# VectorE in written order while the expert weights are prepared, an expert every 9 clock units, and preference for the early steps of ten chunks

## The chip, the core and the metric

The kernel runs on one core of a Trainium2 chip. That core has five engines with instruction streams of their own: TensorE (PE, matrix products), VectorE (DVE), ScalarE (ACT), GpSimd (POOL) and SyncE (SP, which mostly issues transfers). The streams meet only through semaphores. The metric is the time of one execution on the device, in microseconds (us); smaller is better.

## What is computed

A softmax over seven taps weights a causal sum over the sequence, for each of 8 heads. The result goes through a mixture of 8 experts, one expert a token.

```python
# x (8, 3584, 192), weight_gen (8, 3584, 8 heads, 7 taps)
w = np.exp(weight_gen - np.max(weight_gen, axis=-1, keepdims=True))
w = w / (np.sum(w, axis=-1, keepdims=True) + 1e-09)
out = np.einsum('bshk,bskhg->bshg', w, x_unf)   # x_unf: the last 7 rows of each token
...
# x is now out as (28672, 192); w_gate (192, 8), w1 (8, 192, 1024), w2 (8, 1024, 192)
logits = x @ w_gate
expert_idx = np.argmax(logits, axis=1)
gate_w = softmax(logits)[np.arange(N), expert_idx]
for e in range(E):
    h = np.maximum(x_sorted[lo:hi] @ w1[e], 0.0)
    y_sorted[lo:hi] = h @ w2[e]
return gate_w[:, None] * y
```

## The kernel before

The 28672 tokens are cut into 28 chunks of 1024 (8 tokens in each of 128 partitions). A chunk goes through these steps:

- **sums** (L660): softmax of the tap weights (`soft0` to `soft3`) and the weighted sum. For chunks 0 to 2 VectorE makes the products of six of the eight token columns (L354, 1152 wide) and PE adds them up in PSUM by a product with the identity (L363), while POOL does the other two columns alone. From chunk 3 on VectorE does products (L354) and additions (L378) of all columns, 13 passes of 1536.
- **split** (L640): `high` rounds the sum to 16 bits on ACT (L444 or L448) and `low` forms the rest (L461 and L463 on VectorE, or L451 to L453), then 24 transposes on PE (L473), copied out by ACT (L475).
- **finish** (L647): the gate's logits on PE (L485), read by VectorE (L492) and reduced to the expert choice (`route1`, up to L507), ranks on PE (L512, L514), `gate` and `places` on VectorE (L521 to L544), and the scatter of the 1024 rows to the experts' queues in DRAM by POOL (L559). At last `choose` (L568 to L605) selects which full tiles of which expert are ready. Its row numbers are read by SP.

An expert tile (`experts`, L754) reads rows of one expert by a transposing transfer (L743) and that expert's prepared weights, 1.8 MB (L745), and does two layers on PE (L805, L711) with ACT and VectorE between them. Tiles of chunks 1 to 4 have 256 rows: 1 is ready behind chunk 1 and 4 each behind chunks 2, 3 and 4. From chunk 6 on a tile has 384 rows. Tiles come in a fixed order, 97 in all. In the tiles of chunks up to 4 VectorE has no part (L814 and L820 on ACT); later it has one in two tiles of three (L828).

Before the first tile the weights of all experts are prepared, three experts in flight (`PROB` = 3). An expert's raw weights are loaded (L239 to L242), their norms formed on PE (L261) and reduced on VectorE (L262), which is `w_norm`. `w_high` sums over partitions on PE (L268), makes the scale on VectorE (L209 to L212, L270) and the 16-bit part on ACT (L271, L272). `w_low` makes the remainder on VectorE (L278, L280), stores all to `wq` in DRAM (L285 to L290) and then loads the expert three further on into the same buffers. Their memory is given to the tiles' buffers afterwards, and a tile's weights come from `wq`, so no tile starts before the last expert is stored.

The order of the program is written by one loop with a clock of its own, `vector_step` (L907): it takes the next due piece of the tiles' VectorE work, of the weights (`weights`, L868: expert e is due at `W_AT + W_GAP * e`, its later steps 4 and 8 units later), of a chunk's finish, of its split, or else of the sums. A framework then builds the instruction streams from that program. Inside `tc.manual_schedule` with VectorE named, VectorE keeps the written order. Outside, and for all other engines, a scheduler may put a later instruction first when its model finds the earlier one not ready; `tc.high_priority()` gives the instructions inside it preference in that choice. Before the change the stage of the weights (L958) is outside, and the tiles' stage (L960 on) inside; preference goes to the finish of every chunk (`route`) and to nothing else.

Of the kernel before, what the change touches and what calls it, by code (L numbers as in the profile page):

```python
# [46 lines left out]
SHRINK = 1.0 - 2.0 ** -11  # L47
FETCH = 16.0
W_AT = 10.0
W_GAP = 11.0  # L50
W_HIGH = 4.0
W_LOW = 8.0
T_MAIN = 384
# [3 lines left out]
EXP_AT = 4  # L57
SC_AT = 7
MX_FROM = 3
SQ = 4  # L60
PROB = 3
TV = 2
# [51 lines left out]
def conv_moe_kernel(ctx: ExitStack, tc: tile.TileContext, x, wgen, w_gate, w1, w2, out):  # L114
# [203 lines left out]
    def soft0(c):  # L318
        k = ch[c]
        mx = cw.tile([P, J * H], F32, name="mx")  # L320
        nc.vector.tensor_reduce(mx, k.w, axis=AX.X, op=ALU.max)  # L321
        nc.gpsimd.tensor_tensor(k.w, k.w, mx.unsqueeze(2).to_broadcast([P, J * H, KW]), op=ALU.subtract)  # L322

    def soft1(c):
        nc.scalar.activation(ch[c].w, ch[c].w, AF.Exp)
# [80 lines left out]
    def square(c, n, m):  # L406

        k = ch[c]

        def one(half, i, col, m):  # L410
            junk = cw.tile([P, m * D], BF16, name="junk", bufs=1, padded_shape=[P, J * D])
            v = k.x[:, col:col + m, :].rearrange("p a d -> p (a d)")
            nc.scalar.activation(junk, v, AF.Square, accum_out=ssqs[:, half, i:i + 1])  # L413

        if c == 0 and n == 0:
            one(1, 0, 0, HALO)
        one(c % 2, n // 2, HALO + n, m)
# [242 lines left out]
    def sums():  # L660
# [9 lines left out]
        for c in range(NCH):  # L670
# [4 lines left out]
            for cost in taps(c):  # L675
                n += 1
                if n <= 2 and c + 1 < NCH:
                    for i in range(4 * n - 4, 4 * n, SQ):
                        square(c + 1, i, SQ)
                yield cost, None  # L680
                if c + 1 < NCH:
                    if n == 2 and c + 1 < MX_FROM + 2:
                        soft0(c + 1)
                        yield 0.6, None
                    if n == EXP_AT:
                        soft1(c + 1)
                    if n == MX_AT and MX_FROM <= c < NCH - 2:

# [179 lines left out]
    def weights(pro):  # L868

        ev = []  # L870
        for e in range(E):
            at = W_AT + W_GAP * e
            ev += [(at, e, 0), (at + W_HIGH, e, 1), (at + W_LOW, e, 2)]
# [15 lines left out]
    wstream = [None, 0.0]  # L889
# [2 lines left out]

    def advance(queue_, what, after):
        at, g, c = queue_[0]
        with tc.high_priority() if what == "route" else nullcontext():
            lat = next(g, None)
        if lat is None:
            done[what] = c
            queue_.pop(0)
            if after:  # L900
                after(c)
        else:
            lat, cost = lat if isinstance(lat, tuple) else (lat, OP)
            clock[0] += cost
            queue_[0][0] = clock[0] + lat

    def vector_step():  # L907
# [12 lines left out]
        if routes and routes[0][0] <= now + (HURRY if routes[0][2] < SOON else 0.0):  # L920
            clock[0] = max(now, routes[0][0])
            advance(routes, "route", None)
            return True
# [22 lines left out]
    with tc.tile_pool(name="pro", bufs=PROB) as pro, tc.tile_pool(name="pro1", bufs=1) as pro1:  # L946
        stats = [pro1.tile([P, 2], F32, name=f"st{e}") for e in range(E)]
        stage = [pro1.tile([P, W_STAGE], F16, name=f"ws{i}") for i in range(PROB)]
        for t in stage:
            nc.gpsimd.memset(t[:, W_INV:W_INV + 16], 0.0)  # L950
        load(0)
        for e in range(len(stage)):
            w_load(e, pro)
            if e == 0:
                load(1)
        wstream[0] = weights(pro)
        clock[0] = 5.0
        while wstream[0] is not None:  # L958
            vector_step()
    with tc.manual_schedule(engines={mybir.EngineType.DVE}):  # L960
        ffw = ctx.enter_context(tc.tile_pool(name="ffw", bufs=3, reuse_waits="tile"))
        ffx = ctx.enter_context(tc.tile_pool(name="ffx", bufs=2, reuse_waits="tile"))
# [41 lines left out]
```

## Time and profile before

| | |
|---|---|
| median of 3 runs | 1240.84 us (1239.42 to 1244.1) |
| the profiled execution | 1242.18 us, span 1240.5 us |
| PE busy | 1133.4 us, 91% of the span |
| VectorE busy | 1036.7 us, 84% |
| ACT, POOL busy | 696.8 us, 660.6 us |
| mean DMA rate | 259 GB/s over the span |

Busy PE means that some product was in its pipeline, not that it ran at its peak. The span counts from the first instruction that the profile shows to the last; the time of an execution has some 1.7 us more. The chain that ended last lies on PE for 63% of the span and on VectorE for 13%. In the profile's slices of 31 us PE stands at 2 and 1 tenths from 93 to 155 us. The rows used are in the section on the trace below.

### The profile page before, as it was taken

To read this page: it belongs to the slowest core of one execution; us is meant where nothing else is said; L and a number is where in the kernel's file an instruction comes from. 1 tells how busy PE (TensorE), PEld (TensorE's weight loads), DVE (VectorE), ACT (ScalarE), POOL (GpSimd) and SP (SyncE) were. 2 spreads that over 40 slices of the span, in tenths; PEclk is the share of its full clock that TensorE was granted. 3 is DMA by queue.
4 is the path that set the end of the run, shared out by engine and by line. 5 is a ranking of instruction groups with operands and counts; after the bars stand their busy time and mean duration, and the time that the engine had idled before them with its cause. 6 is when DMAs were issued, how large, how long until landed. Compare 5 with 4: busy or idle time off the path is not lost.

```text
span 1240.5 us, 30087 instructions
## 1 busy us (share of the span) xinstructions
PE 1133.4 (91%) x11621; PEld 927.2 (75%) x11621; DVE 1036.7 (84%) x1849; ACT 696.8 (56%) x1459; POOL 660.6 (53%) x562
## 2 busy tenths in 40 slices
PE   5692189997999999999999999999999998999997
PEld 3461179896678788778788787787777786789997
DVE  7999966999999999999999999999998976232331
ACT  3455167675566666656756666656655663543442
POOL 6850853666656565446755565656464656222222
PEclk9896599999999999999999999999999999999998
DMA  9996698897768878787798878878776667999995
GB/s 277 346 323 241 232 282 264 287 304 236 232 201 267 265 230 250 238 234 235 247 277 237 237 227 255 247 240 254 239 215 178 191 197 222 340 348 348 321 362 218
DMA packets 185133, 320.93 MB, mean 259 GB/s; under 512 B 132752, under 2 KB 156434, under 8 KB 169118
## 3 DMA queue, kind: packets, MB, share of 16 engines
q1 hardware_dynamic: 162862, 273.68, 70.8%
q0 software_dynamic: 22128, 45.33, 11.1%
q8 instruction: 91, 1.49, 0.5%
q14 instruction: 52, 0.43, 0.1%
HBM read 236.17 MB, written 60.76 MB: 239 GB/s over the span
## 4 chain that ended last, share of the span: by engine, by line
PE 63%; DVE 13%; DMA 10%; issue 7%; POOL 4%; SPq 1%; ACT 1%; POOLq 0%; DVEq 0%; ACTq 0%
PE ph L805 29%; PE y L711 27%; DVE tv L354 4%; DVE acc L378 3%; DMA wt<-wq 3%; PE ph L473 2%; PE ph L818 2%; DMA f<-in_moe_w_dram 2%; POOL out_dram L559 2%; DMA xt<-queue 2%; DMA queue<-pl,pos 2%; DVE hl L828 1%; POOL queue L559 1%; PE ph L363 1%; PE pm L485 1%
## 5 line engine op out<-in xcount | busy, mean ns | idle before, releaser
L805 PE MATMUL ph<-xt,wt 128*128 128x384 f16 (+6 forms) x3880 | 578.8, 292 | 24.5 <-DMA wt<-wq 16.8
L711 PE MATMUL y<-wt,hh 128*128 128x192 f16 (+2 forms) x3696 | 504.5, 247 | 2.1 <-ACT o L715 2.1
L559 POOL DMA_INDIRECT out_dram<-o,meta x231 | 288.5, 1249 | 394.6 <-ACT o L715 349.0
L711 PE MATMUL y<-wt,hl 128*128 128x192 f16 (+2 forms) x1848 | 450.3, 247 | 0.4 <-ACT hl L820 0.2
L805 PEld LDWEIGHTS <-wt 128*128 128x128 f16 x3880 | 329.3, 98 | 144.4 <-DMA wt<-wq 18.9
L711 PEld LDWEIGHTS <-hh 128*128 128x128 f16 (+2 forms) x3696 | 337.0, 99 | 35.9 <-issue 5.0
L559 POOL DMA_INDIRECT queue<-pl,pos x224 | 286.8, 1280 | 118.1 <-issue 56.7
L828 DVE SCALAR_TENSOR_TENSOR hl<-ph,hh 128x384 f16<-128x384 f32 (+2 forms) x372 | 204.2, 562 | 144.2 <-ACT hh L825 139.0
L354 DVE TENSOR_TENSOR tv<-x_sb,wp 128x1536 f32<-128x1536 f32 (+1 forms) x171 | 289.0, 1693 | 3.9 <-PE ph L363 3.7
L825 ACT ACTIVATE hh<-ph 128x384 f16<-128x384 f32 (+2 forms) x372 | 185.5, 501 | 181.0 <-PE ph L805 170.4
L378 DVE TENSOR_TENSOR acc<-acc,tv 128x1536 f32<-128x1536 f32 x150 | 261.8, 1745 | 0.0
L711 PEld LDWEIGHTS <-hl 128*128 128x128 f16 (+2 forms) x1848 | 181.7, 98 | 16.5 <-ACT hl L820 1.4
L814 ACT ACTIVATE hh<-ph 128x384 f16<-128x384 f32 (+1 forms) x204 | 105.2, 518 | 84.7 <-PE ph L805 82.0
L715 ACT ACTIVATE o<-y,fac 128x192 f32<-128x192 f32 (+2 forms) x231 | 91.7, 418 | 89.4 <-PE y L711 83.4
L820 ACT ACTIVATE hl<-ph 128x384 f16<-128x384 f32 (+1 forms) x204 | 104.1, 519 | 37.0 <-PE ph L818 36.4
L475 ACT ACTIVATE xg<-ph 128x1024 f16<-128x1024 f16 x84 | 83.9, 1027 | 24.3 <-PE ph L473 24.2
L473 PE MATMUL ph<-idh,pl 128*128 128x128 f16 x672 | 56.1, 225 | 25.4 <-ACT pl L448 15.8
L818 PE MATMUL ph<-hh,negi 128*128 128x384 f16 (+1 forms) x256 | 68.1, 304 | 1.7 <-ACT hh L814 1.6
L473 PEld LDWEIGHTS <-pl 128*128 128x128 f16 x672 | 44.5, 101 | 29.4 <-ACT pl L448 16.1
L363 PE MATMUL ph<-tv,identf 128*128 128x384 f32 x126 | 51.6, 553 | 7.6 <-DVE tv L354 7.3
L413 ACT ACTIVATE junk<-x_sb 128x768 bf16<-128x768 f32 (+2 forms) x56 | 48.0, 857 | 13.6 <-DMA x_sb<-in_x_dram 6.5
L322 POOL TENSOR_TENSOR w_sb<-w_sb,mx 128x448 f32<-128x448 f32 x28 | 29.7, 1062 | 45.5 <-DVE mx L321 43.6
(121 smaller groups left out, 780.7 us busy)
## 6 DMA issues: line engine op xcount, KB each, us to landing
wt<-wq SPq DMA_DIRECT2D x97, 1796.0 KB
x_sb<-in_x_dram SPq DMA_DIRECT2D x27, 1344.0 KB
w_sb<-in_weight_gen_dram SPq DMA_DIRECT2D x28, 224.0 KB
wq<-ws SPq DMA_DIRECT2D x8, 772.0 KB
f<-in_moe_w_dram SPq DMA_DIRECT2D x8, 768.0 KB
f<-in_moe_w_dram SPq DMA_DIRECT2D x8, 512.0 KB
wq<-ws SPq DMA_DIRECT2D x8, 512.0 KB
wq<-ws SPq DMA_DIRECT2D x32, 128.0 KB
```

Of the source, the lines that this page charges most:

```text
L354: eng.tensor_tensor(out, xs, ws, op=ALU.mult)
L378: eng.tensor_tensor(ac, ac, t, op=ALU.add)
L473: nc.tensor.transpose(pt[:, m, :], p16[:, j, n * P:(n + 1) * P], idh)
L559: st = nc.gpsimd.indirect_dma_start(out=dst, out_offset=bass.IndirectOffsetOnAxis(ap=idx, axis=0), in_=src, in_offset=None, **kw)
L711: nc.tensor.matmul(y, hx[:, f, sl], w2v[:, f, t, :], start=(f == 0 and k == 0), stop=(f == NF - 1 and k == 2))
L715: nc.scalar.activation(o[0:m, :], y, AF.Copy, scale=fac[0:m, s:s + 1])
L805: nc.tensor.matmul(ph[:, g], wt[:, wc + f * P:wc + (f + 1) * P], xt[:, xc, 0:T], start=(k == 0 and g == 0), stop=(k == 4), skip_group_chec ...
L814: nc.scalar.activation(hv, ph, AF.Relu, scale=SHRINK)
L818: nc.tensor.matmul(ph[:, g], negi, hv[:, g], start=False, stop=True, skip_group_check=True)
L820: nc.scalar.activation(lv, ph, AF.Relu)
L825: nc.scalar.activation(hv, ph, AF.Relu)
L828: nc.vector.scalar_tensor_tensor(lv, ph, 0.0, hv, op0=ALU.max, op1=ALU.subtract)
```

## The change

Three things change: `W_GAP` goes from 11 to 9 units of the loop's clock, so that the expert's steps are due earlier between the chunks' steps; the stage of the weights goes under `tc.manual_schedule` for VectorE, so that VectorE keeps the written order there too; and the split of chunks 0 to 9 gets the preference that the finish had alone. The finish had it already for all chunks.

```diff
--- before.py
+++ after.py
@@ -47,7 +47,7 @@
 SHRINK = 1.0 - 2.0 ** -11
 FETCH = 16.0
 W_AT = 10.0
-W_GAP = 11.0
+W_GAP = 9.0
 W_HIGH = 4.0
 W_LOW = 8.0
 T_MAIN = 384
@@ -57,6 +57,7 @@
 EXP_AT = 4
 SC_AT = 7
 MX_FROM = 3
+FRONT = 10
 SQ = 4
 PROB = 3
 TV = 2
@@ -892,7 +893,7 @@
 
     def advance(queue_, what, after):
         at, g, c = queue_[0]
-        with tc.high_priority() if what == "route" else nullcontext():
+        with tc.high_priority() if what == "route" or c < FRONT else nullcontext():
             lat = next(g, None)
         if lat is None:
             done[what] = c
@@ -955,8 +956,9 @@
                 load(1)
         wstream[0] = weights(pro)
         clock[0] = 5.0
-        while wstream[0] is not None:
-            vector_step()
+        with tc.manual_schedule(engines={mybir.EngineType.DVE}):
+            while wstream[0] is not None:
+                vector_step()
     with tc.manual_schedule(engines={mybir.EngineType.DVE}):
         ffw = ctx.enter_context(tc.tile_pool(name="ffw", bufs=3, reuse_waits="tile"))
         ffx = ctx.enter_context(tc.tile_pool(name="ffx", bufs=2, reuse_waits="tile"))
```

In the built programs VectorE has the same instructions. From the last row of chunk 3's choose on, its list is the same in both; ahead of that the same rows stand in another order. The line numbers of the changed program are one higher behind line 59, two higher at the end.

On VectorE, the stretch in which the logits of chunk 0 are read (`lg`, L492 before, L493 after; `ws` rows are an expert's remainder, `st` its norms, `tv` conv products, `pl` a chunk's payload). Before, expert 3's rows and two conv chunks lie around and between the steps:

```order
L278 SCALAR_TENSOR_TENSOR ws_177<-f_358,nsc,ws_177 128x1536
L343 TENSOR_TENSOR wp<-w_sb,sm 128x336
L492 TENSOR_REDUCE lg<-pm 128x64
L280 SCALAR_TENSOR_TENSOR ws_177<-f_359,nsc,ws_177 128x8x192
L354 TENSOR_TENSOR tv<-x_sb,wp 128x1152
L461 TENSOR_TENSOR pl_133<-acc,pl_133 128x2x128
L463 TENSOR_TENSOR pl_133<-acc,pl_133 128x2x64
L495 TENSOR_REDUCE lm<-lg 128x8
L354 TENSOR_TENSOR tv<-x_sb,wp 128x1152
L262 TENSOR_REDUCE st_173<-y 128x2
L497 TENSOR_TENSOR lg<-lg,lm 128x64
```

After the change the same read stands right behind expert 1's two rows and expert 2's norms:

```order
L355 TENSOR_TENSOR tv<-x_sb,wp 128x1152 x2
L279 SCALAR_TENSOR_TENSOR ws_178<-f_200,nsc,ws_178 128x1536
L281 SCALAR_TENSOR_TENSOR ws_178<-f_201,nsc,ws_178 128x8x192
L263 TENSOR_REDUCE st_171<-y 128x2
L493 TENSOR_REDUCE lg<-pm 128x64
L496 TENSOR_REDUCE lm<-lg 128x8
L498 TENSOR_TENSOR lg<-lg,lm 128x64
L502 SCALAR_TENSOR_TENSOR pri<-lg,revE 128x64
L210 TENSOR_SCALAR nbits<-y 128x2
L212 TENSOR_SCALAR nsc<-nbits 128x2
L213 TENSOR_SCALAR nin<-nbits 128x2
```

The read of chunk 0's logits moved from behind expert 3's L278 to behind expert 1's L281, and its following steps stand next to each other with expert 2's scale among them.

On VectorE, the end of the weights' stage (`f_943` and `f_854` are the raw weights of the last expert). Before, the conv passes of chunk 3 (`acc`) are finished and chunk 4's have begun:

```order
L278 SCALAR_TENSOR_TENSOR ws_178<-f_942,nsc,ws_178 128x1536
L378 TENSOR_TENSOR acc<-acc,tv 128x1536
L343 TENSOR_TENSOR wp<-w_sb,sm 128x448
L584 TENSOR_TENSOR eq<-cand,top 1x64
L497 TENSOR_TENSOR lg<-lg,lm 128x64
L280 SCALAR_TENSOR_TENSOR ws_178<-f_943,nsc,ws_178 128x8x192
L354 TENSOR_TENSOR acc<-x_sb,wp 128x1536
L587 TENSOR_TENSOR eq<-eq,rowc 1x64
L600 TENSOR_SCALAR cand<-cand,top 1x64
L501 SCALAR_TENSOR_TENSOR pri<-lg,revE 128x64
```

After, chunk 3 has begun its conv only, chunk 2's payload stands before the last expert's rows and its logits behind them:

```order
L355 TENSOR_TENSOR acc<-x_sb,wp 128x1536
L462 TENSOR_TENSOR pl_133<-acc,pl_133 128x2x128
L464 TENSOR_TENSOR pl_133<-acc,pl_133 128x2x64
L468 TENSOR_TENSOR lsc<-isx,nin 128x1
L322 TENSOR_REDUCE mx<-w_sb 128x64
L355 TENSOR_TENSOR tv<-x_sb,wp 128x1536 x2
L279 SCALAR_TENSOR_TENSOR ws_178<-f_853,nsc,ws_178 128x1536
L281 SCALAR_TENSOR_TENSOR ws_178<-f_854,nsc,ws_178 128x8x192
L493 TENSOR_REDUCE lg<-pm 128x64
L496 TENSOR_REDUCE lm<-lg 128x8
```

Ten conv passes of chunk 3 moved behind the last expert's rows, and chunk 1's choose in front of them.

On ACT, the copies of the first chunk that comes after the first expert tile has begun (`hh`, `hl` and `o` belong to tiles, `fac` stands once in each tile). Before, this is chunk 4 (`pl_132`), in the third tile:

```order
L325 ACTIVATE w_sb<-w_sb 128x448
L715 ACTIVATE o<-y,fac 128x192
L820 ACTIVATE hl<-ph 128x2x256
L842 ACTIVATE fac<-meta,wt 128x2
L814 ACTIVATE hh<-ph 128x2x256
L448 ACTIVATE pl_132<-acc 128x4x192 x2
L814 ACTIVATE hh<-ph 128x2x256 x2
```

After, it is chunk 3 (`pl_131`), in the second tile:

```order
L821 ACTIVATE hl<-ph 128x2x256 x3
L326 ACTIVATE w_sb<-w_sb 128x448
L815 ACTIVATE hh<-ph 128x2x256 x2
L716 ACTIVATE o<-y,fac 128x192
L821 ACTIVATE hl<-ph 128x2x256 x2
L449 ACTIVATE pl_131<-acc 128x4x192 x2
L716 ACTIVATE o<-y,fac 128x192
```

Chunk 3's copies moved from ahead of the first tile into the second; chunk 4's, further on, moved from behind 2.25 tiles to behind 5. On PE the ranks of chunk 3 stand behind 3.0 tiles (none before), those of chunk 4 behind 7.25 (5.33), of chunk 5 behind 9.75 (8.22), of chunk 6 behind 11.75 (11.05), and of chunk 7 behind 13.5 in both.

## Rows read from the trace of the kernel before

**Rows 1.** The profile's page, busy tenths of TensorE and VectorE in 40 equal slices of 31.0 us.

```profile
PE   5692189997999999999999999999999998999997
...
DVE  7999966999999999999999999999998976232331
```

**Rows 2.** The table by stretch: from and to in us, length, then busy time and number of instructions of PE, PE's weight loads, VectorE, ACT and POOL, and last the granted clock of PE as a share of full speed, the DMA share and GB/s. Eleven stretches of 31 us, and one short stretch from another such table.

```profile
0.00:31.00 31.00, 16.54 (x82) 10.94 (x82) 22.42 (x52) 10.79 (x16) 20.12 (x46) 1.00 0.92 277
31.00:62.00 31.00, 21.18 (x113) 12.67 (x112) 30.78 (x40) 15.32 (x26) 25.29 (x24) 0.84 1.02 346
62.00:93.00 31.00, 28.98 (x211) 19.13 (x210) 29.37 (x52) 16.79 (x26) 15.66 (x14) 0.99 1.01 323
93.00:124.00 31.00, 7.02 (x105) 5.80 (x103) 31.00 (x52) 16.44 (x23) 2.98 (x4) 0.67 0.69 241
124.00:155.00 31.00, 4.79 (x66) 4.03 (x66) 30.41 (x72) 5.02 (x7) 26.36 (x16) 0.50 0.67 232
155.00:186.00 31.00, 27.87 (x264) 24.42 (x264) 20.14 (x20) 18.91 (x39) 15.50 (x15) 0.95 0.95 281
186.00:217.00 31.00, 30.67 (x350) 28.60 (x351) 21.19 (x39) 22.55 (x44) 9.50 (x8) 1.00 0.88 265
217.00:248.00 31.00, 28.57 (x330) 26.41 (x328) 29.30 (x46) 20.51 (x41) 21.50 (x15) 1.00 0.85 285
248.00:279.00 31.00, 30.45 (x350) 28.26 (x349) 29.63 (x48) 22.50 (x45) 20.01 (x16) 1.00 0.93 305
279.00:310.00 31.00, 22.23 (x248) 18.73 (x247) 29.99 (x52) 17.58 (x36) 19.83 (x16) 0.92 0.80 237
310.00:341.00 31.00, 28.90 (x259) 21.38 (x256) 31.00 (x56) 17.29 (x36) 18.74 (x13) 0.92 0.71 233
...
57.00:60.00 3.00, 3.00 (x5) 1.77 (x6) 3.00 (x4) 0.00 (x0) 2.92 (x4) 0.50 0.95 272
```

**Rows 3.** The timeline of PE: start and duration in us, engine, line and operation, output<-inputs, number of instructions in the row, and in brackets the idle time before it and what ended that. L363 are the conv taps that go through PE, L261 the norms of one weight half, L805 the first layer of an expert tile.

```profile
23.75 2.18 PE L363 MATMUL ph<-tv,identf 128*128 128x384 f32 x6
...
56.92 6.95 PE L363 MATMUL ph<-tv,identf 128*128 128x384 f32 x12 [3.00 <-DVE tv L354]
...
100.78 0.86 PE L261 MATMUL y<-f 128*128 128x128 bf16 x12 [0.57 <-DMA f<-in_moe_w_dram]
...
155.27 5.08 PE L805 MATMUL ph<-xt,wt 128*128 128x256 f16 x32 [9.99 <-DMA wt<-wq]
...
201.08 1.26 PE L805 MATMUL ph<-xt,wt 128*128 128x256 f16 x10
```

**Rows 4.** The timeline of VectorE, with the same columns. L280 is the last weight row of an expert (expert 1 and expert 7 here), L605 the last row of chunk 3's choose, L461 the first row of chunk 4's low part, L492 the read of a chunk's logits (chunk 4 at 196, chunk 7 at 288 us).

```profile
47.86 2.63 DVE L280 SCALAR_TENSOR_TENSOR ws<-f,nsc,ws 128x1536 f16<-128x1536 f32 x1
...
127.75 1.80 DVE L280 SCALAR_TENSOR_TENSOR ws<-f,nsc,ws 128x1536 f16<-128x1536 f32 x1
...
148.88 0.15 DVE L605 SCALAR_TENSOR_TENSOR posn<-cnt,posn 1x8 f32<-1x8 f32 x1
...
177.52 0.69 DVE L461 TENSOR_TENSOR pl<-acc,pl 128x512 f16<-128x512 f32 x1 [10.76 <-ACT pl L448]
...
196.15 0.29 DVE L492 TENSOR_REDUCE lg<-pm 128x64 f32<-128x128 f32 x1 [9.81 <-PE pm L485]
...
288.10 0.29 DVE L492 TENSOR_REDUCE lg<-pm 128x64 f32<-128x128 f32 x1 [1.01 <-PE pm L485]
```

**Rows 5.** VectorE's groups by line and shape from 0 to 155 us: names, shapes, count, then busy us and mean ns of one, and idle time before them.

```profile
L354 DVE TENSOR_TENSOR tv<-x_sb,wp 128x1152 f32<-128x1152 f32 x21 | 28.2, 1346 | 3.8 <-PE ph L363 3.7
L354 DVE TENSOR_TENSOR tv<-x_sb,wp 128x1536 f32<-128x1536 f32 x11 | 19.2, 1744 | 0.0
...
L378 DVE TENSOR_TENSOR acc<-acc,tv 128x1536 f32<-128x1536 f32 x9 | 15.7, 1739 | 0.0
...
L330 DVE TENSOR_REDUCE sm<-w_sb 128x64 f32<-128x448 f32 x5 | 3.0, 611 | 0.0
```

**Rows 6.** The timeline of SP's queue (issues of transfers, with the time that an issue took). L285 is the first store of an expert's prepared weights (expert 0 here), L286 one of the last (expert 7 here), L242 the last load of an expert's raw weights (expert 3 and expert 7), L743 the read of a tile's rows, L745 of its weights.

```profile
31.34 0.40 SPq L285 DMA_DIRECT2D wq<-ws  x1
...
39.82 0.56 SPq L242 DMA_DIRECT2D f<-in_moe_w_dram  x1
...
91.91 0.66 SPq L242 DMA_DIRECT2D f<-in_moe_w_dram  x1
...
129.97 0.38 SPq L286 DMA_DIRECT2D wq<-ws  x1
144.14 1.33 SPq L743 DMA_TRANSPOSE xt<-queue  x1
145.95 0.39 SPq L745 DMA_DIRECT2D wt<-wq  x1
```

**Rows 7.** The timeline of POOL: the first scatter of chunk 1 and the last of chunk 3, of 24 that follow each other.

```profile
124.07 6.35 POOL L559 DMA_INDIRECT queue<-pl,pos  x1 [8.74 <-ACT ws L272]
...
166.83 0.96 POOL L559 DMA_INDIRECT queue<-pl,pos  x1 [0.30 <-issue]
```

**Rows 8.** The chain of work that ended last, in two stretches: start and duration in us, and what. The first two rows are the landing of chunk 2's scatters and the read of the second tile's rows; the third is the first layer of the eighth tile.

```profile
155.36 5.98 DMA queue<-pl,pos
161.34 3.18 DMA xt<-queue
...
228.01 2.25 PE ph L805 x19
```

## The prediction

> **What bounds the kernel now.** I read the slices of the page first [rows 1]: TensorE (PE) is nearly empty in the fourth and fifth slice (93 to 155 us) and stays at 8 or 9 from the eleventh to the last but one, while VectorE (DVE) is full from the second to the fifth. The table by stretch says it in numbers [rows 2]: from 93 to 155 us PE works 11.8 of 62 us and DVE 61.4. No expert product runs before 155.27 us [rows 3]. From 155 to 341 us PE idles 17.3 us (six rows summed); DVE idles 20.7 us in the first two of these rows and 4.1 us in the other four. So three stretches follow each other: DVE's front, a middle in which DVE sets the pace after two waits of its own, and PE's long run. The end moves by as much as the start of the long run moves.
>
> One milestone is enough to measure that. From the last row of chunk 3's choose (L605) on, DVE's list is the same row for row in both programs, and on PE chunk 7's logits stand behind 13.0 expert tiles in both. So I ask when DVE reads chunk 7's logits: at 288.10 us now [rows 4].
>
> **Part 1: work that leaves the weights' stage.** Call T the end of the last expert's L280, the last weight row on DVE: 127.75 + 1.80 = 129.55 us [rows 4]. Up to it stand 198 DVE rows now and 181 in the changed program. Ten full conv passes of chunk 3 move behind T (four L354, six L378, each 1.74 us less 0.07 of overlap [rows 5]: 16.7 us), with them twelve small rows of chunks 2, 4 and 5 (2.9 us; five of them up to 0.6 each [rows 5]), and five small rows of chunk 1's choose move ahead of it (0.7 us). Net 18.9 us. With the waits of before T would be 110.6 us.
>
> **Part 2: waits that the written order adds.** DVE idles 10.4 us up to T now (8.6, 0.2, 1.6 and 0 in the first four rows of [rows 2]), since the scheduler nearly always had another row ready. In the written order DVE stands at each row until its input is there. Walking its list against those of PE, ACT and the queue, I find four places.
> (a) Chunk 0's taps. PE takes 2.0 us a tap (2.18 less overlap [rows 3]), DVE 1.3 [rows 5], with two buffers between them. Now weight rows fill the gaps; in the new list few small rows stand there. +2 us.
> (b) Chunk 0's logits. DVE reads them right behind expert 1's L280, and on PE they stand behind expert 3's norms, whose load is issued only after expert 0's store. Issuing store and load takes from 31.34 to 40.4 us now [rows 6], and a load lands some 9 us later (issued at 91.91 [rows 6], awaited by PE until 100.78 [rows 3]). DVE stands 4 us.
> (c) Chunk 2's first tap stands on PE behind expert 5's norms, and ACT's pass for expert 4 behind transposes that wait for the same load. +2 us.
> (d) Chunk 2's fourth tap stands on PE behind expert 7's norms, whose load follows expert 4's store. +5 us; nothing if the load lands 5 us sooner, 8 if it lands 3 later.
> After such gaps PE's clock falls: after 3.00 us without work two taps took 6.95 us at 56.92 [rows 3], and the granted clock from 57 to 60 us was 0.50, its lower level [rows 2]. Another 2 us over all. Sum 15 us; T = 110.6 + 15.4 = 126 us, 3.5 sooner than now. By bounds: 113 with none of (b) to (d) and no slow clock, 138 with loads 4 us later at three of these places.
>
> The Trainium skill ("DMA: Bandwidth & Descriptors", Issuing engines are not separate DMA queues) says that transfers of all issuing engines run on the same 16 DMA engines and interleave. The trace agrees: the DMA share is 1.02 and 1.01 from 31 to 93 us [rows 2]. It speaks against the change, since the same weights have to move in less time. From rows alone: 38.1 MB have moved at 129.55 us (31 us each at 277, 346, 323 and 241 GB/s, 5.55 at 232 [rows 2]), 8.6 of them before 31 us; one chunk's input, about 1.3 MB, falls behind T. The other 28.2 MB at 335 GB/s, the mean of the two full rows, take 84 us. So T is not under 115 us, and this bound stands above the 113.
>
> **Part 3: the first expert tile.** Now it starts 25.7 us after T. SP issues the last store at 129.97 us, then waits until 144.14 for chunk 1's scatters, which GpSimd issues from 124.07 on; the weights go out at 145.95 and PE starts 9.3 us later [rows 3, 6, 7]. In the new program chunk 1's steps stand ahead of expert 5's L278, so this wait is gone. I put 2 us for the store's last issues, 4 for its landing (between 0 and the 9 of a load), 9.3 for the weights: PE starts at T + 15 = 141 us, 14 us sooner.
>
> **Part 4: DVE from T to the end of chunk 3's choose.** Now 149.03 - 129.55 = 19.5 us [rows 4]; the moved 18.9 us come on top: T + 38.4. Two waits are new, since expert work now starts ahead of chunk 3's steps. On ACT chunk 3's copies stand behind the first half of the second tile. That tile needs chunk 2's scatters: T + 2 for the positions, 15 for eight scatters (the 24 from 124.07 to 167.8 us take 1.82 each [rows 7]), 6.0 and 3.2 for their landing and for the rows' read [rows 8]: T + 26. Half a tile and the passes queued ahead add 3.5; DVE reaches L461 at T + 24.5 and stands 5 us. On PE chunk 3's ranks stand behind 3.0 tiles (none now): 1.5 us more. L605 ends at T + 45 = 171 us, 22 us later than now.
>
> One of those scatters took 6.35 us, the last 0.96 [rows 7]. At 0.96 with 0.3 between them eight take 10 us, the wait at L461 is gone and the sum is 5 us smaller; I keep the mean, as conv passes run beside them as now. The Trainium skill ("SBUF — State Buffer", SBUF: two separate sides) knows a lock that fits the long one: GpSimd cannot write descriptors while VectorE holds the port pair that they share.
>
> **Part 5: what is taken away.** DVE's two long waits, 10.76 us for ACT's copies of chunk 4 and 9.81 us for its logits [rows 4], go: chunk 4's copies stood behind expert tiles that themselves waited for weights. In the new program these copies stand behind 5.0 tiles; now those end at 202.3 us, 47 after the first starts [rows 3], so then at 188. DVE wants them 17.7 us after L605 (149.03 to 177.52 less the wait), at 189: I take 1.5 us for the copies themselves. Chunk 4's ranks stand behind 7.25 tiles, now at 229 us [rows 8], 74 after the start, so then at 215, as DVE gets there: 1 us. Chunk 5's logits cost 1 more. From there PE is some 11 us ahead of DVE's need, and the two waits for chunk 6's and 7's logits, 1.3 and 1.0 us (the latter in [rows 4]), go.
>
> **Sum.** For the milestone: +22 (part 4) - 20.6 + 1.5 + 1 + 1 - 2.3 (part 5) = +2.6 us. T decides: the milestone shifts by T less 123.4 us. The profiled execution took 1242.18 us (span 1240.5), so 1244.8 in its terms; the median of the runs is 1240.84, 1.3 lower: 1243.
>
> **Rivals.**
> First, the earlier start carries through (faster). If loads land early, T falls towards its bound of 115 us and PE starts at 130. Then the milestone comes 8 us sooner, 1232; without the wait at L461 too, 1227. For it: DMA's share is 0.92 before 31 us [rows 2], so there is some room, and the lower bound of (d) is nothing. Against it: PE's lead alone is worth nothing while DVE, with 4.1 us of idle time from 217 to 341, is the later one. It decides at T = 117. Chance 0.28.
> Second, the load chain sets the pace (slower). A load goes out only after the store of the expert three before, and DVE, bound to its list, cannot use the gap. Expert 1's L280 ends at 50.5 us now [rows 4] and, by the walk, then; the other six take 13.2 us each now. At 14.5 T is 137.5, the milestone 14 us later: 1255. For it: DVE was 98% busy from 31 to 155 us only by its free order [rows 2]. Its places are (b) and (d); it decides at T = 129.6. Chance 0.29.
> Third, the change hardly does what it says. The lists are alike behind chunk 3, so it acts on 170 of 1240 us only; if the lead and the waits cancel, the end is within 3 us of now. That is part of "no change".
>
> **How the numbers follow.** About 0.5% (6.2 us) is what a measurement of this kernel can tell from no change. The forecast is no change, 1243 us, with 0.43: T between 117 and 129.6 gives 1234 to 1247. The range that should hold 8 in 10 reaches to 1229 (T at its bound, half of L461's wait gone) and to 1257 (T = 137.5 and the tiles 2 us late). Faster by over 0.5%: 0.28; slower: 0.29.
>
> **What would show it.** The last weight row on DVE ends near 126 us, PE's first expert product comes near 141; DVE waits 3 to 6 us for chunk 0's logits near 51 us and again for chunk 2's taps near 103; chunk 3's choose ends near 171; the waits for chunk 4's copies and logits are under 4 us together; chunk 7's logits are read near 291. I am wrong if the last is off by more than 6 us, or if the time moves and it does not.

## The result and the profile after the change

The changed kernel takes 1252.6 us, median of 5 runs (1249.66 to 1255.72); the ratio to the kernel before is 1.0098, with a 95% interval from 1.0076 to 1.0119. The change costs 1.0%. The time lies inside the forecast's range of 1229 to 1257 us, but "no change" at 1243 did not come. The profiled execution has a span of 1253.9 us against 1240.5.

The page's busy tenths of PE and VectorE (DVE) in 40 equal slices, here of 31.3 us; they answer to [rows 1]:

```profile
PE   5675598787899999999999999999999998999997
...
DVE  6788897989999999999999999999998976133331
```

The hole in PE's fourth and fifth slice is half filled (5 and 5 in place of 2 and 1), but the five slices from the seventh on, nearly all at 9 before, stand at 7 and 8. DVE, at 9 from the second to the fifth slice before, stands at 7 and 8 there.

DVE's timeline after the change, as in [rows 4]: start, duration, line, and in brackets the idle time before a row and what ended it. L493 at 54.78 reads chunk 0's logits, L281 is the last weight row, L606 ends chunk 3's choose; then come chunk 4's low part (L462), logits (L493) and the sum of its exponentials (L522), chunk 5's low part and ranks (L536), and chunk 7's logits:

```profile
54.78 0.29 DVE L493 TENSOR_REDUCE lg<-pm 128x64 f32<-128x128 f32 x1 [5.83 <-PE pm L486]
...
104.96 1.35 DVE L355 TENSOR_TENSOR tv<-x_sb,wp 128x1152 f32<-128x1152 f32 x1 [2.50 <-PE ph L364]
...
123.71 1.81 DVE L281 SCALAR_TENSOR_TENSOR ws<-f,nsc,ws 128x1536 f16<-128x1536 f32 x1
...
171.01 0.15 DVE L606 SCALAR_TENSOR_TENSOR posn<-cnt,posn 1x8 f32<-1x8 f32 x1
...
192.54 0.69 DVE L462 TENSOR_TENSOR pl<-acc,pl 128x512 f16<-128x512 f32 x1 [3.66 <-ACT pl L449]
...
201.28 0.28 DVE L493 TENSOR_REDUCE lg<-pm 128x64 f32<-128x128 f32 x1
...
213.86 0.22 DVE L522 TENSOR_REDUCE se<-eg 128x8 f32<-128x64 f32 x1 [4.27 <-ACT eg L499]
...
228.33 0.69 DVE L462 TENSOR_TENSOR pl<-acc,pl 128x512 f16<-128x512 f32 x1 [2.23 <-ACT pl L449]
...
259.34 0.23 DVE L536 TENSOR_TENSOR rk<-pm,nb 128x64 f32<-128x64 f32 x1 [5.77 <-PE pm L515]
...
302.55 0.28 DVE L493 TENSOR_REDUCE lg<-pm 128x64 f32<-128x128 f32 x1
```

Chunk 7's logits are read 14.45 us later than in [rows 4], and the span is 13.4 us longer: the milestone carries the result. From it to the end of the span both kernels take nearly the same, 952.4 us before and 951.4 after. Of the 14.45 us, 10.4 are idle time of DVE; the other 4.0 are busy time, for the same rows (last section). The table by stretch (DVE's busy time is the third pair of numbers) shows where DVE lost time, up to the last weight row, on to chunk 3's choose, to chunk 4's logits, and to chunk 5's positions. Before:

```profile
0.00:129.55 129.55, 74.00 (x508) 48.64 (x508) 119.12 (x199) 61.17 (x93) 69.53 (x86) 0.86 0.91 299
129.55:149.03 19.48, 4.50 (x65) 3.92 (x65) 18.89 (x60) 3.20 (x4) 15.79 (x13) 0.50 0.50 154
149.03:196.15 47.12, 37.80 (x392) 33.76 (x393) 26.45 (x28) 25.75 (x50) 22.49 (x18) 0.90 0.95 304
196.15:243.89 47.74, 45.35 (x510) 42.22 (x509) 47.74 (x81) 32.11 (x66) 27.15 (x18) 1.00 0.84 253
```

After:

```profile
0.00:125.52 125.52, 80.36 (x507) 53.11 (x508) 101.03 (x182) 57.22 (x85) 73.50 (x92) 0.82 0.93 301
125.52:171.16 45.64, 29.66 (x303) 25.80 (x303) 40.02 (x77) 21.08 (x40) 16.47 (x14) 0.77 0.91 279
171.16:201.28 30.12, 28.11 (x321) 25.94 (x319) 26.36 (x28) 19.66 (x40) 17.73 (x13) 1.00 0.82 232
201.28:262.67 61.39, 47.72 (x479) 41.93 (x477) 49.12 (x82) 32.79 (x67) 26.15 (x19) 0.89 0.72 234
```

Length less busy time is DVE's idle time: 10.4, 0.6, 20.7 and 0.0 us before; 24.5, 5.6, 3.8 and 12.3 us after. For the last of these eight the forecast had 2 us. PE and the chain of waits say what it is. PE after the change, the first expert product and the two stands in that stretch:

```profile
140.40 6.58 PE L806 MATMUL ph<-xt,wt 128*128 128x256 f16 x32 [12.86 <-DMA wt<-wq]
...
208.91 1.46 PE L806 MATMUL ph<-xt,wt 128*128 128x256 f16 x6 [4.93 <-DMA wt<-wq]
...
250.38 5.98 PE L806 MATMUL ph<-xt,wt 128*128 128x256 f16 x30 [6.11 <-DMA xt<-queue]
```

ACT at the first stand. That tile is the seventh. L815 is its first pass; L821 are the last two low passes of the sixth tile, whose products (L819) stand on PE behind the seventh tile's first ones; L499 are chunk 4's exponentials:

```profile
210.84 0.60 ACT L821 ACTIVATE hl<-ph 128x512 f16<-128x512 f32 x1 [5.79 <-PE ph L819]
211.69 0.60 ACT L815 ACTIVATE hh<-ph 128x512 f16<-128x512 f32 x1 [0.26 <-PE ph L806]
...
213.01 0.59 ACT L821 ACTIVATE hl<-ph 128x512 f16<-128x512 f32 x1
213.49 0.34 ACT L499 ACTIVATE eg<-lg,lsc 128x64 f32<-128x64 f32 x1
```

The chain of waits (start, duration, what) at both:

```profile
194.91 13.96 DMA wt<-wq
...
229.13 2.60 POOL queue L560
...
243.04 3.55 DMA queue<-pl,pos
...
246.85 3.40 DMA xt<-queue
250.38 5.98 PE ph L806 x30
...
259.12 0.20 PE pm L515 x8
259.34 0.23 DVE rk L536
```

GpSimd (POOL) before chunk 4's scatters:

```profile
227.84 0.98 POOL L560 DMA_INDIRECT out_dram<-o,meta  x1 [3.46 <-ACT o L716]
229.13 2.60 POOL L560 DMA_INDIRECT queue<-pl,pos  x1 [0.30 <-DVE pl L462]
```

It is a loop. The seventh tile waits for its weights, which took 13.96 us; chunk 4's exponentials stand on ACT behind that tile's first pass, so DVE stands 4.27 us and forms chunk 4's positions late, at 224.10 (213.50 before). GpSimd's stream has a tile's output rows ahead of chunk 4's scatters and waits for them, so the scatters start at 229.13, 4.8 us behind the positions (before the change 0.4 us, at 214.08); a tile that needs these rows gets them at 250.25; chunk 5's ranks stand on PE behind this tile's first products, and DVE stands 5.77 us again.

### The profile page after: what moved, and what is told of

Its sections match the earlier page's. It is cut to its first block, busy times and chain, and to the rows that moved or that the text cites. A ratio compares the mean times of both kernels' runs of the same rounds, so it can differ in the third digit from the quotient of the medians.

```text
span 1253.9 us, 30093 instructions
## 1 busy us (share of the span) xinstructions
PE 1146.8 (91%) x11621; PEld 934.2 (75%) x11621; DVE 1040.7 (83%) x1849; ACT 698.5 (56%) x1459; POOL 653.5 (52%) x562
## 4 chain that ended last, share of the span: by engine, by line
PE 60%; DMA 15%; issue 9%; DVE 9%; POOL 4%; ACT 2%; SPq 1%; POOLq 0%; DVEq 0%; ACTq 0%
PE ph L806 29%; PE y L712 25%; DMA wt<-wq 4%; DMA f<-in_moe_w_dram 3%; POOL out_dram L560 2%; DVE tv L355 2%; DMA queue<-pl,pos 2%; PE ph L474 2%; DMA wq<-ws 2%; PE ph L819 2%; POOL queue L560 2%; DVE hl L829 1%; DVE acc L379 1%; DMA meta<-queue 1%; PE ph L364 1%
## 5 line engine op out<-in xcount | busy, mean ns | idle before, releaser
L806 PE MATMUL ph<-xt,wt 128*128 128x384 f16 (+6 forms) x3880 | 586.4, 295 | 41.0 <-DMA wt<-wq 22.1
L560 POOL DMA_INDIRECT out_dram<-o,meta x231 | 283.0, 1225 | 400.8 <-ACT o L716 361.4
L806 PEld LDWEIGHTS <-wt 128*128 128x128 f16 x3880 | 333.4, 99 | 165.0 <-issue 23.3
L560 POOL DMA_INDIRECT queue<-pl,pos x224 | 282.8, 1262 | 121.6 <-issue 66.0
L815 ACT ACTIVATE hh<-ph 128x384 f16<-128x384 f32 (+1 forms) x204 | 105.2, 518 | 82.3 <-PE ph L806 79.6
L821 ACT ACTIVATE hl<-ph 128x384 f16<-128x384 f32 (+1 forms) x204 | 104.0, 518 | 42.0 <-PE ph L819 41.3
L819 PE MATMUL ph<-hh,negi 128*128 128x384 f16 (+1 forms) x256 | 69.0, 306 | 2.0 <-ACT hh L815 1.9
L449 ACT ACTIVATE pl<-acc 128x768 f16<-128x768 f32 (+1 forms) x53 | 41.0, 821 | 21.4 <-DVE acc L379 15.1
```

What stands on the lines that cost most here:

```text
L560: st = nc.gpsimd.indirect_dma_start(out=dst, out_offset=bass.IndirectOffsetOnAxis(ap=idx, axis=0), in_=src, in_offset=None, **kw)
L806: nc.tensor.matmul(ph[:, g], wt[:, wc + f * P:wc + (f + 1) * P], xt[:, xc, 0:T], start=(k == 0 and g == 0), stop=(k == 4), skip_group_chec ...
L815: nc.scalar.activation(hv, ph, AF.Relu, scale=SHRINK)
L819: nc.tensor.matmul(ph[:, g], negi, hv[:, g], start=False, stop=True, skip_group_check=True)
L821: nc.scalar.activation(lv, ph, AF.Relu)
```

## Experiments

The diffs are against the changed kernel. **Theory A** says that the loss lies in these waits around chunks 3 to 5; **theory B** says that it lies in the 14 us which the written order adds up to the last weight row. The chips of e5 to e12 needed 1364.5 us for the kernel before (e1 to e4: 1241.5); PE's stream has pauses there, from about 250 us on (last section). So of those runs I read the ratio to the kernel before on the same chip, and the trace only up to chunk 5's positions. The changed kernel itself was not run on these chips.

**e1, the written order alone.**

```diff
-W_GAP = 9.0
+W_GAP = 11.0
...
-        with tc.high_priority() if what == "route" or c < FRONT else nullcontext():
+        with tc.high_priority() if what == "route" else nullcontext():
```

> Only the written order in the weights' stage; W_GAP stays 11 and no preference for the split. On PE chunk 3's ranks stand behind 1.25 tiles (3.0 after the change, none before), chunk 4's behind 5.5 (7.25, 5.33), chunk 5's behind 8.5 (9.75, 8.22). Theory A (the harm of the change is the new waits of VectorE around chunks 3 to 5, whose steps stand behind tiles that wait for rows): the waits of the weights' stage come in full (some 24 us of idle time up to the last expert's end, near 135 us), chunk 3's choose ends near 165, but the waits of chunks 4 and 5 are nearly gone, chunk 7's logits are read near 284 and the end is near 1237 us, 0.3% below before. Theory B (the waits that the written order adds in the weights' stage go through to the end, whatever stands behind): chunk 7's logits near 302, the end near 1254.

Measured: 1246.12 us, ratio 1.0032 (1.0013 to 1.0052). The row up to the last weight row:

```profile
0.00:140.84 140.84, 80.34 (x516) 54.07 (x516) 116.23 (x214) 59.24 (x90) 80.29 (x99) 0.81 0.86 275
```

24.6 us idle, as after the change; yet chunk 7's logits are read at 291.28, not 302. Theory B falls: DVE's later arrival takes away the two long waits of before. Theory A is nearer, but 7 us too low at the logits and 9 at the end, which it had 0.3% below before: the last weight row came at 140.84, not 135, chunk 3's choose at 169.2, not 165, and 6.3 us of waits remained from there to chunk 7's logits.

**e2, W_GAP 9 alone.**

```diff
-        with tc.manual_schedule(engines={mybir.EngineType.DVE}):
-            while wstream[0] is not None:
-                vector_step()
+        while wstream[0] is not None:
+            vector_step()
...
-        with tc.high_priority() if what == "route" or c < FRONT else nullcontext():
+        with tc.high_priority() if what == "route" else nullcontext():
```

> Only W_GAP 9; the weights' stage stays with the scheduler, no preference for the split. On PE chunk 3's ranks stand behind 2.5 tiles, chunk 4's behind 6.75, chunk 5's behind 9.75, nearly as after the change. Theory A: VectorE idles some 10 us up to the last expert's end (near 116 to 121 us), chunk 3's choose ends near 157, but the waits of chunks 3 to 5 come as after the change or longer (16 to 25 us from there to chunk 7's logits, since VectorE arrives sooner and the tiles don't): logits near 293 to 298, the end near 1248 us. Theory B: the 14 us of waits in the weights' stage are what was lost, so that without them chunk 7's logits are read near 288 and the end is that of before, 1241.

Measured: 1238.03 us, ratio 0.9961 (0.9937 to 0.9985): faster.

```profile
0.00:114.47 114.47, 73.90 (x516) 48.86 (x516) 103.42 (x200) 56.69 (x86) 72.84 (x91) 0.93 0.98 322
114.47:160.82 46.35, 26.14 (x267) 22.84 (x268) 36.97 (x59) 20.23 (x37) 18.72 (x15) 0.74 0.90 283
```

Both theories were too high in the time. The last weight row ends 11 us sooner than after the change, and the loop does not form, though chunk 5's ranks stand behind 9.75 tiles in both: the two rows have 11.1 and 9.4 us of idle time, and from chunk 3's choose to chunk 5's positions 6.1 us. So the number of tiles ahead on PE does not decide alone. Of the 7.9 us that chunk 7's logits come sooner only 2.0 are left at the end.

**e3, tiles written 20 units later.**

```diff
-START = 20.0
+START = 40.0
```

> The change as it is, with START 40 in place of 20, so that the tiles are written 20 clock units later against the chunks' steps. VectorE's list up to chunk 6's logits is the same; on PE chunk 3's ranks stand behind 1.25 tiles (3.0 after the change), chunk 4's behind 5.25 (7.25), chunk 5's behind 8.0 (9.75), chunk 6's behind 10.75 (11.75). Theory A: the weights' stage is as after the change (last expert near 125.5, first tile near 140); the 15.9 us of waits between chunk 3's choose and chunk 7's logits fall to 3 to 6 us, the logits are read near 290 and the end is near 1242. Rival (PE is the late one there: a tile that starts later only moves the loss from VectorE to PE): the waits go but PE idles more by as much, and the end stays near 1252.

Measured: 1250.80 us, ratio 1.0071 (1.0046 to 1.0096). The waits went (1.9 us from chunk 3's choose to chunk 5's positions) and chunk 7's logits are read at 285.89, as theory A says; but the end did not follow, as the rival says. The place of the loss is later. From 600 to 900 us, e3 and then the changed kernel:

```profile
600.00:900.00 300.00, 294.10 (x2892) 234.18 (x2891) 285.62 (x501) 182.59 (x400) 172.76 (x134) 0.99 0.76 237
```

```profile
600.00:900.00 300.00, 299.17 (x2963) 238.32 (x2961) 297.78 (x529) 187.36 (x410) 181.35 (x138) 1.00 0.80 246
```

DVE does 12 us less there. My reading is that tiles written later stay later for the whole run; e5 tests it.

**e4, chunk 0's finish 8 units later.**

```diff
-            advance(splits, "split", lambda c: routes.append([clock[0], finish(c), c]))
+            advance(splits, "split", lambda c: routes.append([clock[0] + (8.0 if c == 0 else 0.0), finish(c), c]))
```

> The change as it is, with chunk 0's finish due 8 clock units later, so that VectorE forms two conv products and expert 2's scale before it reads chunk 0's logits. The wait of 5.8 us at this read goes to under 1.5 us. Theory B: what VectorE saves there it keeps, since the conv work between chunk 3 and 7 follows directly: last expert near 121, chunk 3's choose near 166, chunk 7's logits near 298, the end near 1248. Theory A: the steps of chunks 4 and 5 still wait for tiles that stand for rows and weights, and give back at least half of it: the end 1250 to 1253. Third possibility: the load of expert 3 and what hangs on it sets the pace of the weights' stage, and the last expert's end stays at 125.

Measured: 1241.67 us, ratio 1.0002 (0.9986 to 1.0018). The whole loss is gone.

```profile
0.00:126.25 126.25, 76.80 (x507) 52.37 (x508) 102.14 (x182) 56.86 (x85) 70.51 (x92) 0.85 0.93 299
...
201.22:250.54 49.32, 45.22 (x516) 42.41 (x513) 49.32 (x81) 34.55 (x71) 24.56 (x20) 1.00 0.81 280
```

Not for the reason of the edit: the wait at chunk 0's logits fell to 2.9 us, but others took its place, and the last weight row ends at 126.25 (the third possibility). Chunk 4's logits are read at 201.22, as after the change. From there on DVE has no idle time where it had 12.3 us, and chunk 7's logits come 12.1 us sooner. The edit also shifted chunk 4's exponentials on ACT a few rows forward, ahead of the seventh tile's first pass. But by e4's own rows that place alone costs little. In e4 the seventh tile finds its weights there when PE comes to it, and the passes that stood ahead of the exponentials after the change end at 209.29, when DVE wants the exponentials at 209.46:

```profile
207.38 2.35 PE L806 MATMUL ph<-xt,wt 128*128 128x256 f16 x20
...
208.70 0.59 ACT L815 ACTIVATE hh<-ph 128x512 f16<-128x512 f32 x1
...
209.46 0.21 DVE L522 TENSOR_REDUCE se<-eg 128x8 f32<-128x64 f32 x1
```

With the 0.33 us of the exponentials themselves, the old place would have cost about 0.2 us here (an estimate from these rows), not 4.27. SP's queue shows a difference in the issues of the seventh and the eighth tile's weights, after the change and in e4:

```profile
194.91 0.34 SPq L746 DMA_DIRECT2D wt<-wq  x1
...
200.42 0.33 SPq L746 DMA_DIRECT2D wt<-wq  x1
```

```profile
195.22 0.34 SPq L746 DMA_DIRECT2D wt<-wq  x1
...
207.45 0.34 SPq L746 DMA_DIRECT2D wt<-wq  x1
```

After the change both reads are under way together. That this makes the seventh late is not tested.

**e5 and e9, tiles 20 units later up to the twelfth** (one kernel, two chips).

```diff
-START = 20.0
+START = 40.0
...
             n, _ = parts.send(True)
+            if n == 12:
+                clock[1] -= 20.0
```

> As e3 (the change, tiles written 20 clock units later), but the 20 units are taken back behind the twelfth tile, so that from chunk 8 on the order on PE is that of the change. What e3 gained up to chunk 7's logits (285.9 us against 302.6 after the change) should now reach the end: from these logits to the end before, after and e4 took 952.4, 951.4 and 952.4 us in their profiles. By the theory that VectorE's waits behind tiles that stand for rows and weights are the loss: logits near 286, VectorE's idle time from chunk 3's choose to there near 4.5 us, end near 1239. By the rival (PE is the late one, and a tile that starts later costs as much): logits near 286, end near 1250 as in e3.

> The kernel of e5 once more, since e5's chip put pauses into PE's stream that stand in no other run. Expected as for e5. Theory (VectorE's waits behind tiles that stand for rows and weights are the loss): chunk 7's logits near 286 us, end near 1239. Rival (PE is the late one): logits near 286 and the end near 1250 as in e3.

Measured: 0.9999 (0.9959 to 1.0040) and 1.0028 (0.9994 to 1.0062). Both intervals hold 1, so without e3's late part most of the 1.0% seems regained. It is not shown: e7 below, which has the loop, has an interval on such a chip that overlaps both. In e9 DVE idles 3.1 us from chunk 3's choose to chunk 5's positions; chunk 7's logits come at 291.64, not 286.

**e10, tiles 10 units later up to the twelfth.**

```diff
-START = 20.0
+START = 30.0
...
             n, _ = parts.send(True)
+            if n == 12:
+                clock[1] -= 10.0
```

> The change, with tiles written 10 clock units later up to the twelfth, and nothing else. On ACT chunk 4's exponentials then stand behind 5 tiles and chunk 5's behind 8 (6 and 9 after the change), as in e4; on PE chunk 4's ranks behind 6.0 and chunk 5's behind 9.0 (7.25 and 9.75). Chunk 0's finish stays where the change has it, with its wait of 5.8 us. If e4 gained by the place of these steps: the last expert near 125, chunk 7's logits near 290, end near 1242. If e4 gained by the wait at chunk 0's logits that it took away: logits near 302, end near 1252.

Measured: 1.0057 (1.0019 to 1.0095). The front keeps its wait at chunk 0's logits (5.29 us) and the last weight row at 126.90; the stretch behind chunk 4's logits:

```profile
199.67:247.90 48.23, 44.06 (x502) 41.25 (x499) 48.06 (x82) 33.49 (x69) 26.15 (x20) 1.00 0.85 255
```

0.2 us idle in place of 12.3: chunk 5's positions come 14.8 us sooner than after the change. So chunk 0's wait is not the cause. The seventh tile does not wait for its weights here either. The edit moves the steps' places and the tiles' times together, so it doesn't say which of the two counts. Its end is not settled: that interval holds neither 1.0002 nor the ratio of the change, and e7, with the loop, has 1.0064 on a like chip, though chunk 5's positions come 13.7 us later there (261.60).

**e6 and e12, the preference alone** (one kernel, two chips).

```diff
-W_GAP = 9.0
+W_GAP = 11.0
...
-        with tc.manual_schedule(engines={mybir.EngineType.DVE}):
-            while wstream[0] is not None:
-                vector_step()
+        while wstream[0] is not None:
+            vector_step()
```

> Only the preference for the split of the first ten chunks; W_GAP 11, scheduler in the weights' stage. Ten conv passes of chunk 3 stand ahead of the last expert's rows on VectorE as before, and chunk 4's ranks stand behind 5.0 tiles (5.33 before). By the theory that the preference acts on a few rows only: chunk 7's logits within 4 us of before's 288.1, end 1237 to 1245. By the rival that the preference causes part of the harm (splits taken ahead of weight rows): last expert's end 5 us later and the end over 1247.

> The kernel of e6 once more, for the same reason. Only the preference for the split. If it acts on a few rows only: chunk 7's logits within 4 us of 288.1, end 1237 to 1245. If it costs by itself, as e6's ratio of 1.006 says: VectorE waits for taps near 77 to 84 us, where it takes conv products early, last expert 4 us later or more, end over 1246.

Measured: 1.0059 (1.0025 to 1.0093) and 1.0063 (1.0039 to 1.0087): slower, which I had not expected at first. In e12 the last weight row ends at 132.1 (129.55 before) and chunk 5's positions come at 246.0 (243.9). In e6 it is 136.1 and 250.0, 6 us later than before, as the rival said. The 2 us of e12 are a quarter of 0.6%; where the rest goes the pauses hide.

**e7, the change without the preference.**

```diff
-        with tc.high_priority() if what == "route" or c < FRONT else nullcontext():
+        with tc.high_priority() if what == "route" else nullcontext():
```

> The change without its preference: W_GAP 9 and the written order. VectorE's list is that of the change row for row; on PE, ACT and POOL a few neighbours stand the other way round. By the theory that the preference does nothing here: last expert's end near 125.5, chunk 7's logits near 302, end near 1252. Rival: the waits of chunks 4 and 5 hang on small things, as e4 showed (4.9 us in place of 16.1 with nearly the same front), so a swap of neighbours on ACT or PE can give the end of e4, 1242.

Measured: 1.0064 (1.0019 to 1.0109), a wide interval, which the ratio of the change lies in. The four waits of the loop are there at the same places, 3.65, 3.27, 1.76 and 5.26 us. Beside the other two parts the preference does nothing that these runs show.

**e8 and e11, W_GAP 9 alone with tiles 10 units later up to the twelfth** (one kernel, two chips; e2's edit and e10's).

```diff
-START = 20.0
+START = 30.0
...
+        while wstream[0] is not None:
+            vector_step()
...
+            if n == 12:
+                clock[1] -= 10.0
```

> A version made from what helped: e2 (W_GAP 9 only), with tiles written 10 clock units later up to the twelfth, so that chunk 3's logits and ranks stand behind 1.25 and 1.75 tiles in place of 2.0 and 2.5. In e2 VectorE waited 8.5 us for these two and 6.1 us more up to chunk 7's logits. By the theory: idle time from the last expert to chunk 7's logits falls from 15.5 to about 8 us, logits near 273, end near 1231 to 1233. Rival: PE becomes the bound (in e2 6 of the 8 us that the logits came sooner were lost again behind them), end 1236 to 1239.

> The kernel of e8 once more, for the same reason as e9. W_GAP 9 alone, with tiles 10 clock units later up to the twelfth. Theory: VectorE's idle time from the last expert to chunk 7's logits about 8 us (15.5 in e2), logits near 273, end near 1231 to 1233. Rival (PE becomes the bound): end 1236 to 1239 as e2.

Measured: 0.9916 (0.9879 to 0.9953) and 0.9904 (0.9869 to 0.9939), faster than before and than the change. From the last weight row to chunk 3's choose 1.4 and 1.9 us of idle time are left of e2's 9.4. But from there to chunk 5's positions DVE idles 9.4 us in both, 6.1 in e2, so the theory's 8 us up to chunk 7's logits are passed before chunk 5, and these logits are read near 281, not 273. The end in us on a chip like that of e1 to e4 was not measured.

The kernels in one table, from their profiles (of two runs of one kernel the later): end of the last weight row, chunk 3's choose, chunk 5's positions, DVE's idle time up to the first and between the last two (us), the `fac` rows (one a tile, near the end of its first layer) that stand on ACT ahead of chunk 4's and chunk 5's exponentials, and the ratio, for e7 and e9 to e12 on the chips with pauses:

| | last weight row | choose 3 | positions 5 | idle before | idle behind | `fac` ahead | ratio |
|---|---|---|---|---|---|---|---|
| before | 129.55 | 149.03 | 243.89 | 10.4 | 20.7 | 4, 7 | 1 |
| the change | 125.52 | 171.16 | 262.67 | 24.5 | 16.0 | 6, 9 | 1.0098 |
| e7 no preference | 127.91 | 173.09 | 261.60 | 25.8 | 14.0 | 6, 9 | 1.0064 |
| e1 order | 140.84 | 169.22 | 248.59 | 24.6 | 4.3 | 4, 7 | 1.0032 |
| e3 | 123.86 | 166.47 | 242.36 | 21.1 | 1.9 | 4, 6 | 1.0071 |
| e4 | 126.25 | 169.96 | 250.54 | 24.1 | 4.9 | 5, 8 | 1.0002 |
| e10 | 126.90 | 169.56 | 247.90 | 24.8 | 3.9 | 5, 8 | 1.0057 |
| e9 | 126.20 | 167.93 | 246.12 | 22.7 | 3.1 | 4, 6 | 1.0028 |
| e12 preference | 132.12 | 152.27 | 245.97 | 13.4 | 20.2 | 4, 7 | 1.0063 |
| e2 gap | 114.47 | 160.82 | 240.35 | 11.1 | 6.1 | 5, 8 | 0.9961 |
| e11 | 114.57 | 153.36 | 236.94 | 11.6 | 9.4 | 5, 8 | 0.9904 |

The traces of e6 and e12, one kernel on two chips, lie 4 us apart at the last weight row and at chunk 5's positions, so smaller differences between chips say nothing. In the table every kernel with the written order idles 21 to 26 us up to the last weight row, the others less (10 to 13). Only the two with 6 and 9 have the loop, and only in these two the seventh tile stands on PE for its weights (4.93 and 3.94 us; under 0.9 in the others). Counted by passes (L815) the place differs less: chunk 4's exponentials stand behind 6.25 tiles after the change and in e7, 6.0 in e4 and e2, and chunk 5's behind 9.0 in all four. Before and in the kernel with the preference alone the 20 us were other waits, for a first tile that came late.

## Why the forecast held up to chunk 3 and failed behind it

**Part 1 and 2, right.** T came at 125.52 us, forecast 126. Idle time up to it grew by 14.1 us, forecast 15 (the step to T adds 15.4). The waits after the change were 5.8 us at chunk 0's logits (4 forecast), 4.1 at chunk 2's taps (7) and 2.6 at chunk 0's taps (2); two waits of 1.1 us at later taps and one of 2.0 us at an input were not on the list. So the sum fits better than its terms. What sets the 24 us is not settled: e4 took 3 of the 5.8 us away and T stayed.

**Part 3, right.** First expert product at 140.40, forecast 141.

**Part 4, right.** Chunk 3's choose ended at 171.16, forecast 171; of its terms the wait at the low part was 2.9 us (5), and the work 40.0 (38.4). The eight scatters of chunk 2 went out within 12.5 us, between the bounds of 10 and 15, none over 1.95 us. No run here shows the lock that the Trainium skill ("SBUF — State Buffer", SBUF: two separate sides) offers for the long one.

**Part 5, the failing step.** The two long waits went, 20.6 us, and those of chunks 6 and 7, as forecast. The step "From there PE is some 11 us ahead of DVE's need" failed. It gave 1.5, 1 and 1 us for what remains; measured were 3.66, 4.27, 2.23 and 5.77, 15.9 us in all. It let the tiles run at their old pace from an earlier start, 74 us to chunk 4's ranks; they took 80, since tiles waited for weights. And it left out that a tile waits for rows which DVE itself releases: part 4 had a price, 24 us from the positions to the tile (15, 6.0 and 3.2), and part 5 did not apply it to chunk 4, whose 224.1 gives 248 (measured 250.38). That this price comes near is in part luck: 4.8 us of wait on GpSimd, 16.1 for the scatters, 1.4 to the last landing and 3.4 for the rows' read were measured. The 12.4 us too little make +2.6 into +15.0; the milestone moved by +14.45, to 302.55 in place of 291. The forecast called itself wrong if that was off by more than 6 us; it was off by 11.6.

**The rivals.** The load chain gave 1255 us, near the measured time, by another mechanism: T was 125.5, not 137.5. The range's upper end came from it too, so that 1252.6 lies inside is luck, and "no change", at 0.43, was wrong. The first rival needed T near 115; the tiles' start, 15 us sooner than before, was not carried through. That the change hardly acts behind chunk 3 because the lists are alike was wrong in its reason: an equal list on DVE says nothing on what it waits for.

**The parts of the change.** Order +0.3%, gap -0.4%, both without the preference +0.6% (e7) with the loop, the preference alone +0.6% (e6 and e12). None of the three alone has the loop. That the waits from chunk 4's logits on are the loss is shown by e4: with nearly the same T and the same time of chunk 4's logits it is without the 12.3 us of idle time and without the 1.0%. On the chips with pauses no run shows that the end follows (e7 and e10). What starts the loop is read from the traces alone: the seventh tile's late weights, in the two kernels that have it and in no other. Why they are late, and how much the steps' place on ACT adds, stays open.

## What to carry to other kernels

Where one engine's result releases work that stands ahead of its own next step on another engine, follow the loop once round with its price; a lead at its start is no lead behind the first turn. Follow every stream in it, here GpSimd's too, which had a tile's output ahead of the scatters. Moving a stage's order and its pace together can put steps where neither does alone, so time each part by itself. A milestone behind which the lists are alike (here 952 us to the end in both) turns a 1% question into a reading of a few rows, but check that the tiles' place against the chunks is alike too, as e3 shows.

## What the runs showed of the hardware

**The same program takes 10% longer on some chips.** The kernel before took 1364.5 and 1364.6 us on two of them, 1241.5 on the chip of e1 to e4. On those two PE's weight loads stand without a releaser. PE idles 165.5 us in e11 (66.9 of them up to 250 us) and 103.0 in e2 (69.2), kernels that differ in the place of twelve tiles. The waits of PE's weight loads in e11, and then in e2 on a chip without such pauses (us in total, times, longest):

```profile
PEld L712 <- issue: 48.5, 53, 4.6
PEld L806 <- issue: 39.9, 104, 6.5
```

```profile
PEld L806 <- issue: 19.1, 25, 7.6
...
PEld L712 <- issue: 6.4, 5, 3.1
```

The profile doesn't show what they wait for, and these stands are only a part of the 123 us.

**Small rows that depend on each other don't overlap.** After the change chunk 0's small rows of 0.22 us start 0.26 us apart (55.10, 55.36, 55.62); between conv passes such a row takes 0.13 us (203.15 to the next row at 203.28). DVE's busy time up to chunk 5's positions is 217.5 us in e1 and 212.2 before, while the summed durations of its groups are no longer (238.9 and 239.9 us): the rows overlap less. That the small rows in a row make this difference is likely, not shown.

**One tile's weights took 8.4 to 14.0 us to come** (131.99 and 194.91 us in the chain of waits), 1796 KB each:

```profile
131.99 8.36 DMA wt<-wq
```

The Trainium skill ("DMA: Bandwidth & Descriptors", Issuing engines are not separate DMA queues) says that transfers of all engines interleave on the same 16. The trace agrees: during these two reads the engines moved 317 and 326 GB/s, while 1796 KB in those times make 220 and 132, so both had other traffic beside them. No run here separates what that costs.
